# Three PSUM places shared by second stage, exponents and inverse in an S4 layer, and a new order of its rounds

## The chip, the cores and the metric

The kernel runs on one core of a Trainium2 chip. The metric is device time in microseconds (us) of one execution of the program; of several runs the median counts. The engines of the core work side by side, each through its own queue in order: PE (TensorE, matmuls), DVE (VectorE), ACT (ScalarE), POOL (GpSimd) and SP (SyncE, which here only starts DMAs). They wait for one another by semaphores.

## The reference

One layer: an adaptive layer norm, a state space convolution (S4), a second adaptive layer norm, a gated feed-forward. L = 2048 positions, D = 640 channels, N = 128 states, F = 1728.

```
mod = (silu(c) @ w_mod) split into sa, ca, ga, sb, cb, gb
h = layernorm(x) * (1 + ca) + sa
K[d, l] = Re sum_n C[d,n] * exp(dt[d] * A[d,n] * l) * dt[d] * B[d,n]       # l = 0..2047
y = irfft(rfft(h, 4096) * rfft(K, 4096))[:2048] + h * Dskip                # per channel
x = x + ga * y
h = layernorm(x) * (1 + cb) + sb
x = x + gb * ((silu(h @ w1) * (h @ w3)) @ w2)
```

All of it is in float32; the change lies in the part that makes K and convolves.

## The kernel before, in words

The core has 8 PSUM banks of 128 partitions x 512 floats. In the part at issue they are six places: A, B and Z of two banks each, and two single ones, `pk` and `pb`.

The program has three parts. First come the modulation, the first norm and the first DFT stage of h, which goes to DRAM (`us`); its order is a written list of words, FRONT. Then come the rounds, where K is made and the convolution runs. Then come the second norm and the feed-forward, where PE multiplies nearly without a pause.

The rounds work on 40 steps of 16 channels. What they issue is set by a list of words, ROUND, which is run once for each of 10 rounds; the word `E1+2` in round r issues the piece E1 of step 4r + 2, unless it was issued before. On PE, DVE, ACT and POOL pieces stay in the order of the words. The pieces of a step:

- `PH` (POOL, for two steps): phases, three integer operations on the tile `ph`. `AB`, `CO`, `SI` (ACT, for two steps): absolute value, cosine and sine of them, 128x2048.
- `PA`, `PQ` (PE): exponents of the fast and the slow half, two banks each, tile `pa`; `XA`, `XQ` (ACT): their exponentials, into the table `A`.
- `E1`, `E2`, `A1`, `A2` (DVE): tables times cosine (tile `E`) and times sine (tile `A`), 128x1024 and 128x512.
- `kg` (PE): the 64 small matmuls that give 16 channels of K, in `pk`; `K` (DVE): two operations, the skip term added to a column of `pk` and a product into SBUF; `pt` (PE) and `uk` (ACT): the first DFT stage of K, through `pb`.

A channel chunk of 128 has 8 steps. The convolution runs on 40 groups (5 chunks x 8 groups of frequencies), ten steps behind; group words carry the number of the step beside which they run, so `st10` is the first group and `st49` the last:

- `st` (PE): the second DFT stage of h and K, 16 matmuls into two banks, tile `p2`; `kc` (ACT): copies K's half out of it.
- `T` (two operations on DVE): the products, the second of them written back into `p2`; `Y` (DVE): their sums.
- `iv` (PE): the first inverse stage, 16 matmuls; `zt` (ACT): copies its result out for a store.

Before the change `st` goes to place A (odd groups near the end to B), the exponents of all steps from 12 on go to B, and the inverse of two groups fills Z, from which one `zt` of 128x1024 takes both. The names in the profile are `p` for `p2`, `pz`, `pa`, `pk`, `pt`, `kc`, `zt`. Line 115 is a helper that records nearly every operation, so the rows are told apart by tiles.

Beside the words the round loop loads and sums the last columns of the modulation (`LS`, `LP`, `LC`, `LO`, once in each of rounds 2 to 6), loads four tiles of x (`x_load`), and loads what is stored of the first inverse stage (tiles `A<-zs`, `z_load`, on POOL's queue). After the rounds a loop over `tk` runs the groups 42 to 49. At the end of it the first four tiles of x are finished; in the feed-forward they are stored to DRAM on POOL's queue (`xs<-xm`), while four further tiles are loaded (`x_get`) and finished (`x_mid`) beside the first matmuls.

## Time and profile before

| what | value |
|---|---|
| median of three runs | 930.04 us (928.35 to 930.1) |
| profiled execution | 928.49 us |
| its span | 926.6 us |
| PE busy in the span | 865.7 us, 93% |
| DVE, ACT, POOL busy | 696.6, 541.4, 290.7 us |
| mean granted TensorE clock | 0.97 |

The profiled execution lies 1.89 us above its span: that is what lies around the profiled instructions. In a timeline a row has the start, the duration in us, the engine, and in square brackets the idle time ahead of it and whose signal ended it. In windows each engine has its busy time and its number of instructions in a stretch. A duration runs from start to end of one instruction; where the next one is ready, it starts some 0.1 us before that end.

### The profile page before, as it was taken

The page shows a single profiled execution, that of the slowest core. Times are in us where ns is not written, and L with a number is a line of the kernel's source. Part 1 is how long each engine was busy: PE and PEld are TensorE (multiplying, and loading weights), DVE is VectorE, ACT ScalarE, POOL GpSimd, SP SyncE. Part 2 cuts the span into 40 slices and gives each one's busy share as a digit, 9 for nine tenths or more (in the row PEclk, how much of TensorE's full clock was granted, in tenths as well). Part 3 has the DMA queues.
Part 4 walks back from the last instruction along what each step waited for, and adds up shares of the span by engine and source line. Part 5 has one row for each costly group of instructions (what it writes and reads, how often), then busy time and mean ns, then how long its engine had stood idle before and what let it go on. Part 6 is the DMA issues. An engine that isn't in the chain of part 4 may idle for free.

```text
span 926.6 us, 20179 instructions
## 1 busy us (share of the span) xinstructions
PE 865.7 (93%) x8082; PEld 664.7 (72%) x8082; DVE 696.6 (75%) x1210; ACT 541.4 (58%) x746; POOL 290.7 (31%) x327
## 2 busy tenths in 40 slices
PE   3788979999998899899999999999999999999997
PEld 2545556666666677678888887778888888888886
DVE  5899899999999968667666656777976666664664
ACT  5989889999999643474433333574633333333432
POOL 3333535543545212213222202310422222100563
PEclk9777699999999999999999999999999999999999
DMA  8664475766675977953221129946321322123352
GB/s 264 214 221 174 155 214 170 224 176 190 177 222 172 290 225 222 263 189 100 57 58 57 47 82 244 267 128 202 111 58 45 112 57 58 57 86 99 100 188 97
DMA packets 103329, 140.69 MB, mean 152 GB/s; under 512 B 19940, under 2 KB 62436, under 8 KB 103236
## 3 DMA queue, kind: packets, MB, share of 16 engines
q1 hardware_dynamic: 92532, 113.71, 40.8%
q10 hardware_dynamic: 8272, 18.16, 6.7%
q0 software_dynamic: 2432, 7.54, 2.6%
q8 instruction: 63, 1.03, 0.5%
q14 instruction: 30, 0.25, 0.1%
HBM read 107.92 MB, written 31.46 MB: 150 GB/s over the span
## 4 chain that ended last, share of the span: by engine, by line
PE 77%; DVE 10%; ACT 7%; DMA 3%; issue 3%; SPq 0%; POOL 0%; DVEq 0%; ACTq 0%
PE ps L115 56%; PE p L115 7%; PE pz L115 4%; PE pt L115 3%; PE pk L115 2%; PE pa L115 2%; DVE u L115 2%; DVE A L115 2%; DVE uk L115 1%; ACT A L115 1%; ACT cs L115 1%; ACT uk L115 1%; DVE E L115 1%; DMA s<-in_s_dram 1%; DVE st L115 1%
## 5 line engine op out<-in xcount | busy, mean ns | idle before, releaser
L115 DVE TENSOR_TENSOR s<-ps,s 128x512 f32<-128x512 f32 x138 | 94.8, 687 | 82.4 <-PE ps L115 82.0
L115 ACT CAST gh<-rw 128x640 fp32r<-128x640 f32 x87 | 63.3, 727 | 110.2 <-PE ps L115 90.6
L115 DVE TENSOR_TENSOR gl<-rw,gh 128x640 fp32r<-128x640 f32 x87 | 77.3, 888 | 64.1 <-ACT gh L115 64.1
L115 POOL TENSOR_TENSOR S<-rw 128x256 f32<-128x256 f32 x46 | 35.6, 776 | 233.9 <-DVE S0l L115 156.6
L115 POOL TENSOR_TENSOR ph<-thi,iota 128x1376 int32<-128x1376 int32 x20 | 51.3, 2563 | 117.3 <-DVE A L115 96.0
L115 PE MATMUL ps<-xA,gh 128*128 128x512 f32 x280 | 87.5, 391 | 0.4 <-ACT xA L115 0.4
L115 PE MATMUL ps<-gh,uh 128*128 128x512 f32 x224 | 87.4, 390 | 0.0
L115 PE MATMUL ps<-gl,uh 128*128 128x512 f32 x224 | 87.2, 389 | 0.0
L115 PE MATMUL p<-uk,s 128*64 128x256 f32 x576 | 71.1, 389 | 15.1 <-issue 4.2
L115 DVE TENSOR_TENSOR E<-A,cs 128x1024 f32<-128x1024 f32 (+1 forms) x80 | 81.7, 1033 | 3.1 <-PE pk L115 1.8
L115 PE MATMUL ps<-gh,ul 128*128 128x512 f32 x208 | 81.0, 390 | 0.0
L115 ACT ACTIVATE A<-pa 128x1024 f32<-128x1024 f32 (+1 forms) x80 | 64.2, 815 | 10.1 <-PE pa L115 9.5
L115 PEld LDWEIGHTS p<-uk,s 128*64 128x64 f32 x576 | 41.0, 137 | 36.4 <-DVE Y L115 5.6
L115 PEld LDWEIGHTS ps<-xA,gh 128*128 128x128 f32 x280 | 52.3, 188 | 12.6 <-ACT s L115 1.2
L115 POOL TENSOR_TENSOR rw<-rw,gbr 128x128 f32<-128x128 f32 x56 | 36.8, 691 | 72.5 <-DMA rw<-in_w_dram 71.0
L115 DVE TENSOR_TENSOR A<-A,ph 128x1024 f32<-128x1024 f32 x40 | 54.1, 1356 | 0.8
L115 PE MATMUL ps<-xA,gl 128*128 128x512 f32 x140 | 54.5, 389 | 0.0
L115 PE MATMUL pt<-s,K 128*64 128x128 f32 x640 | 46.5, 290 | 5.5 <-ACT uk L115 5.5
L115 PEld LDWEIGHTS ps<-gh,uh 128*128 128x128 f32 x224 | 42.0, 188 | 9.0 <-DVE h L115 0.2
L115 PEld LDWEIGHTS ps<-gl,uh 128*128 128x128 f32 x224 | 42.1, 188 | 8.8
L115 ACT ACTIVATE s<-ps 128x512 f32<-128x512 f32 (+1 forms) x33 | 19.7, 597 | 47.2 <-PE ps L115 47.2
L115 PEld LDWEIGHTS pt<-s,K 128*64 128x64 f32 x640 | 36.8, 144 | 14.0 <-ACT uk L115 8.8
(224 smaller groups left out, 2210.8 us busy)
## 6 DMA issues: line engine op xcount, KB each, us to landing
rw<-in_w_dram ACTq DMA_DIRECT2D x44, 320.0 KB, 3.1
us<-u SPq DMA_DIRECT2D x16, 640.0 KB, 3.4
rw<-in_wg_dram SPq DMA_DIRECT2D x31, 320.0 KB, 2.9
s<-in_s_dram SPq DMA_DIRECT2D x36, 256.0 KB, 4.6
i<-in_i_dram SPq DMA_DIRECT2D x36, 256.0 KB, 4.3
rw<-in_wu_dram SPq DMA_DIRECT2D x28, 320.0 KB, 3.1
uk<-us SPq DMA_DIRECT2D x16, 512.0 KB, 4.9
zs<-zt SPq DMA_DIRECT2D x16, 512.0 KB, 4.5
```

Of the source, the lines that this page charges most:

```text
L115: ins = fn(*args, **kw)
```

## The change

1. `two_banks` hands out the places A, Z and B. A tile of `st`, `PA`, `PQ` (and three tiles of the end) takes the place whose holder was released first; the holder of an exponent is released by its exponential, that of a second stage by its `zt`.
2. The inverse of a group goes into the first half of its own `p2`, and each group has a `zt` of its own, 128x512 instead of 128x1024 for two; the store still takes two.
3. `T` is split into `T` and `P`, and `K` into `D` and `K`, so that they can be put apart.
4. ROUND is rewritten, and the last rounds have a list of their own, LAST.
5. `x_load` moves from the `E1` words of rounds 7 and 8 to `uk` words of rounds 6 and 7; the first twelve `z_load` move behind the rounds; the four stores `xs<-xm` move behind the last `x_mid`; the scale of the modulation is added when a column is copied.

```diff
-            ps = to[s] = psS.tile([P, 2, 512], F32, name="pa", tag="AB"[s % 2] if s < 12 else "B", bufs=1)
+            if s < 12:
+                ps = psS.tile([P, 2, 512], F32, name="pa", tag="AB"[s % 2], bufs=1)
+            else:
+                ps = two_banks([P, 2, 512], "pa", ("XA" if n == NB else "XQ", s))
+            to[s] = ps
+    banks = {"A": ("zt", LAG), "Z": None, "B": None}
+    used = {}
+    def two_banks(shape, name, release):
+        free = [t for t, r in banks.items() if r is None or r in used]
+        tag = min(free, key=lambda t: used.get(banks[t], -1))
+        banks[tag] = release
+        return psS.tile(shape, F32, name=name, tag=tag, bufs=1)
...
-        p2 = psS.tile([P, 2, 2, 2 * DC], F32, name="p2", tag="B" if n > NS - 12 and n % 2 else "A", bufs=1)
+        if n:
+            p2 = two_banks(shape, "p2", ("zt", n + LAG))
+        Zq[ch, g] = p2[:, :, 0].rearrange("p r (i d) -> p r i d", i=2)
...
-        if g % 2 == 0:
-            Zq[ch] = psS.tile([P, 2, 4, DC], F32, name="pz", tag="Z", bufs=1)
-        pz = Zq[ch]
+        pz = Zq[ch, g]
...
+    def k_direct(s):
+        pk = PK[s]
+        keep(V.tensor_tensor(pk[:, :, 0], pk[:, :, 0], dz[:, s * 4:s * 4 + 4], op=OP.add))
+    def products2(ch, g):
+        p2, kc, T = Pq[ch, g]
+        T2 = p2[:, :, :, DC:]
+        keep(V.tensor_tensor(T2, bc(p2[:, :, 1, :DC], 2, 2), kc[:, :, ::-1, :], op=OP.mult))
...
-            return
-        zt = fp.tile([P, 8, DC], F32, name="zt", bufs=2)
-        acopy(zt.rearrange("p (i r) d -> p r i d", r=2), Zq.pop(ch))
+            ztp[0] = fp.tile([P, 8, DC], F32, name="zt", bufs=2)
+        zt = ztp[0]
+        z_out(zt[:, g % 2 * 4:g % 2 * 4 + 4], ch, g)
...
     ROUND = (
-        "E1+2 pt+0 CO+4 kg+1 A1+2 kc+2 SI+4 T+2 PA+4 uk+0 XA+4 Y+2 E2+2 st+3 K+1 zt+1 kc+3 A2+2 kg+2 "
...
+        "PQ+7 LS+4 LP+4 st+5 A1+4 E2+5 XQ+7 PH+8 LC+4 LO+4 CO+6 A1+5 A2+5 kg+4 pt+3 D+4 kc+5 iv+4 SI+6 uk+3 "
...
+    LAST = (
+        "st+37 XQ+38 D+35 E2+37 kc+37 A1+36 D+33 T+37 E1+36 A1+37 pt+34 PQ+39 pt+35 PQ+36 iv+36 kg+36 A1+34 "
...
-            if name == "E1" and 30 <= k < 38 and k % 2 == 0:
-                x_load((k - 30) // 2)
+            if name == "uk" and 28 <= k < 32:
+                x_load(k - 28)
             if name == "kg" and 36 <= k < 40:
                 early.append((None, z_tile()))
-                z_load(early[-1][1], k - 36, range(3), q=nc.gpsimd)
...
+        if tk <= NS + 4:
+            z_load(early[tk - NS - 1][1], tk - NS - 1, range(3), q=nc.gpsimd)
...
-            if pair == 0 and n == 1:
-                with tc.issue_after(power.ins):
+            if pair == 0 and n == 3:
+                with tc.issue_after(kept_out[0].ins):
                     for j, (x, z, st) in enumerate(early):
                         G.dma_start(xs[j], x)
```

What it moves, at three places. First DVE, in a middle round, behind the `A2` that closes step 15. Before:

```order
L115 SCALAR_TENSOR_TENSOR A<-ph,A 128x16x32
L115 TENSOR_TENSOR T<-p_1823,kc 128x512
L115 TENSOR_TENSOR p_1823<-p_1823,kc 128x4x128
L115 TENSOR_TENSOR Y<-T,p_1823 128x2x128 x2
L115 TENSOR_TENSOR A<-A,ph 128x16x64
L115 TENSOR_TENSOR pk<-pk,dz 128x4
L115 TENSOR_TENSOR K_1998<-pk,gaT 128x256
L115 TENSOR_TENSOR E<-A,cs 128x16x64
L115 TENSOR_TENSOR T<-p_1986,kc 128x512
```

And now:

```order
L115 SCALAR_TENSOR_TENSOR A<-ph,A 128x16x32
L115 TENSOR_TENSOR E<-A,cs 128x16x64
L115 TENSOR_TENSOR T<-p_1822,kc 128x512
L115 TENSOR_TENSOR p_1822<-p_1822,kc 128x4x128
L115 TENSOR_TENSOR pk<-pk,dz 128x4
L115 TENSOR_TENSOR Y<-T,p_1822 128x2x128 x2
L115 TENSOR_TENSOR K_1984<-pk,gaT 128x256
L115 TENSOR_TENSOR E<-A,cs 128x16x64
L115 TENSOR_TENSOR T<-p_1972,kc 128x512
```

The operations are the same; a table product `E` now stands directly behind `A2`, the next `A` behind the products has left this place, and the skip term stands between product and sum.

Then ACT, where a round's sines and cosines are. Before:

```order
L115 ACTIVATE ph<-ph 128x32x64
L115 COPY kc<-p_2440 128x512
L115 ACTIVATE cs<-cs 128x2048
L115 COPY uk<-pt 128x32x16
L115 ACTIVATE cs<-ph 128x2048
L115 ACTIVATE cs<-cs 128x2048
L115 COPY kc<-p_2530 128x512
L115 ACTIVATE ph<-ph 128x32x64
L115 COPY uk<-pt 128x32x16
L115 ACT_TABLE_LOAD
L115 ACTIVATE A<-pa 128x16x2x32
L115 COPY zt<-pz 128x2x4x128
```

And now:

```order
L115 ACTIVATE cs<-cs 128x2048
L115 COPY kc<-p_2040 128x512
L115 ACTIVATE ph<-ph 128x32x64
L115 COPY uk<-pt 128x32x16
L115 ACTIVATE cs<-ph 128x2048
L115 COPY zt<-p_1972 128x2x2x128
L115 COPY kc<-p_2128 128x512
L115 ACTIVATE ph<-ph 128x32x64
L115 COPY zt<-p_2040 128x2x2x128
L115 ACTIVATE cs<-cs 128x2048
L115 ACT_TABLE_LOAD
L115 ACTIVATE A<-pa 128x16x2x32
```

Each long one now has one or two copies behind it, and the copies out of the inverse are single groups out of `p`.

Last PE, around the late columns `pm` of a round. Before:

```order
L115 MATMUL p_2781<-uk,s_2779 64x256 x8
L115 MATMUL pa<-r_98,lx 128x512 x2
L115 MATMUL pz<-Y,i_2796 128x128 x8
L115 MATMUL pa<-r_99,lx 128x256 x2
L115 MATMUL pm<-xw,sc 32x384 x4
L115 MATMUL pm<-xw,sc 32x192 x2
L115 MATMUL p_2838<-uk,s_2836 64x256 x8
```

And now:

```order
L115 MATMUL p_2768<-uk,s_2766 64x256 x8
L115 MATMUL pa<-r_98,lx 128x512 x2
L115 MATMUL pt<-s_74,K_2697 64x128 x8
L115 MATMUL p_2617<-Y,i_2804 128x128 x8
L115 MATMUL pa<-r_99,lx 128x256 x2
L115 MATMUL pm<-xw,sc 32x384 x4
L115 MATMUL pm<-xw,sc 32x192 x2
L115 MATMUL p_2836<-uk,s_2834 64x256 x8
```

The inverse now writes into the tile of its own second stage (`p_2617`), and a `pt` stands ahead of it.

More of the change, by code (lines that the diff above doesn't have):

```diff
@@ L470, in late_out @@
         lo, hi = late_blocks[i]
-        keep(V.tensor_copy(modTf[:, 3 * i + lo:3 * i + hi], pm[:, 384 + lo:384 + hi]))
+        for one in (0, 1):
+            c = [b for b in range(lo, hi) if (KD <= 3 * i + b < 2 * KD) == bool(one)]
+            if c:
+                to, src = modTf[:, 3 * i + c[0]:3 * i + c[-1] + 1], pm[:, 384 + c[0]:384 + c[-1] + 1]
+                keep(V.tensor_scalar(to, src, 1.0, None, op0=OP.add) if one else V.tensor_copy(to, src))
         if i >= 3:
             keep(V.tensor_copy(gbr[:, (i - 3) * 256:(i - 3) * 256 + 256], pm[:, :256]))
-        if i == 4:
-            keep(V.tensor_scalar(modT[:, 1, :], modT[:, 1, :], 1.0, None, op0=OP.add))
     hpz = pre.enter_context(tc.tile_pool(name="hpz", bufs=2, side="right"))
@@ L639, in imag2 @@
         A = AA[s]
-        keep(V.scalar_tensor_tensor(A[:, :, 0, :], ph.pop(s)[:, :, 2 * NA - 1:NA - 1:-1], -1.0, A[:, :, 0, :],
+        keep(V.scalar_tensor_tensor(A[:, :, 0, :], ph[s][:, :, 2 * NA - 1:NA - 1:-1], -1.0, A[:, :, 0, :],
                                     op0=OP.mult, op1=OP.mult))
@@ L722, in stage2 @@
         n = ch * 8 + g
-        p2 = psS.tile([P, 2, 2, 2 * DC], F32, name="p2", tag="B" if n > NS - 12 and n % 2 else "A", bufs=1)
+        shape = [P, 2, 2, 2 * DC]
+        if n:
+            p2 = two_banks(shape, "p2", ("zt", n + LAG))
+        else:
+            p2 = psS.tile(shape, F32, name="p2", tag="A", bufs=1)
+        Zq[ch, g] = p2[:, :, 0].rearrange("p r (i d) -> p r i d", i=2)
         for pi in range(2):
@@ L890, in x_products @@
             if j == 2:
-                pys.append(psS.tile([P, 2, 512], F32, name="py", tag="B", bufs=1))
+                pys.append(two_banks([P, 2, 512], "py", ("py", 0)))
             py = [pys[0][:, hh, (j - 2) * 256:] for hh in range(2)]
@@ L933, in do @@
             assert (name, k) not in done and lo <= k < hi, (name, k)
-        if (name, k) in done or not lo <= k < hi or (name == "zt" and k % 2 == 0 and k < LAG + 8 * NDC - 8):
+        if (name, k) in done or not lo <= k < hi:
             return None
         done.add((name, k))
+        used[name, k] = len(used)
         return (conv if name in conv else parts)[name](k)
@@ L1028, in tile_kernel @@
     ROUND = (
[5 rows of a table removed]
[5 rows of a table added]
+    ).split()
+    LAST = (
[8 rows of a table added]
     ).split()
@@ L1036, in tile_kernel @@
     pieces = {"LS": late_sums, "LP": late_part, "LC": late_cols, "LO": late_out}
-    for rnd in range(NS // EB):
+    for rnd in range(8 + 1):
         if 2 <= rnd < 7:
             late_load(rnd - 2)
-        for word in ROUND:
-            name, k = word[:2].rstrip("+-"), EB * rnd + int(word[len(word[:2].rstrip("+-")):])
+        for word in ROUND if rnd < 8 else LAST:
+            name, k = word.split("+")
+            k = int(k) + (EB * rnd if rnd < 8 else 0)
             if name in pieces:
@@ L1070, in tile_kernel @@
         do("zt", tk - 1)
-        do("T", tk)
-        do("Y", tk)
+        for name in "TPY":
+            do(name, tk)
         if tk == NS + 1:
@@ L1096, in tile_kernel @@
             if i == 6:
-                pl = psS.tile([P, 2, 512], F32, name="pl", tag="A", bufs=1)
+                pl = two_banks([P, 2, 512], "pl", ("pl", 0))
                 pls += [pl[:, 0], pl[:, 1]] + [psS.tile([P, 512], F32, name="pl", tag=t, bufs=1) for t in ("pk", "pb")]
@@ L1103, in tile_kernel @@
                 late_products(7)
-    ps = psS.tile([P, 2, 512], F32, name="ps", tag="Z", bufs=1)[:, 0]
+    ps = two_banks([P, 2, 512], "ps", ("ps", 0))[:, 0]
     for _ in range(IDLE):
@@ L1187, in behind @@
         return tc.issue_after(last.ins) if last else ExitStack()
+    kept_out = [None]
     def x_mid(j, got, g):
```

25 lines of the change are left out of this document (15 added, 10 removed), and 15 rows, old and new, of tables (LAST, ROUND).

## The prediction

> **What bounds the kernel now.** I read the windows first, cut at the same `st` of each round (length, then busy time and instructions of PE, weight loads, DVE, ACT and POOL, then clock, DMA share and GB/s), then the groups by form, then one round in order of time, on DVE beside POOL.
>
> ```profile
> 179.80:206.90 27.10, 25.41 (x484) 18.35 (x486) 25.52 (x43) 25.64 (x27) 13.03 (x7) 1.00 0.67 194
> 234.30:261.40 27.10, 25.50 (x480) 18.09 (x480) 25.87 (x45) 25.65 (x27) 12.98 (x7) 1.00 0.63 182
> 261.40:288.10 26.70, 23.56 (x465) 17.21 (x465) 25.20 (x41) 25.25 (x27) 13.35 (x8) 1.00 0.64 204
> 335.50:366.70 31.20, 31.20 (x465) 21.78 (x466) 23.71 (x60) 11.41 (x20) 8.40 (x16) 1.00 0.70 215
> ```
>
> A round with late columns takes 27.1 us, one without 26.7, and in both three engines are within 1.2 to 3.1 us of full. No order makes a round shorter than its fullest engine: DVE 25.5 to 25.9, ACT 25.6. So a reordering can win about 1.5 us in a round, not more. From 335 us on PE has no gap; what is won before that moves the rest up, and nothing there gives it back.
>
> ```profile
> L115 DVE TENSOR_TENSOR T<-p,kc 128x512 f32<-128x512 f32 x24 | 16.4, 685 | 4.9 <-ACT kc L115 4.9
> L115 ACT ACTIVATE A<-pa 128x1024 f32<-128x1024 f32 x22 | 22.6, 1028 | 4.5 <-PE pa L115 4.5
> L115 ACT COPY kc<-p 128x512 f32<-128x512 f32 x23 | 13.4, 582 | 3.2 <-issue 2.5
> L115 ACT COPY zt<-pz 128x1024 f32<-128x1024 f32 x12 | 12.1, 1011 | 0.3
> L115 ACT ACTIVATE cs<-cs 128x2048 f32<-128x2048 f32 x11 | 21.1, 1915 | 0.2
> L115 PE MATMUL p<-uk,s 128*64 128x256 f32 x368 | 44.8, 385 | 10.6 <-DVE Y L115 3.3 <-ACT uk L115 3.2 <-PE pa L115 1.6
> ```
>
> These groups are from 165 to 320 us. DVE's one large wait is for `kc`, the copy behind a second stage; ACT waits for exponents; PE waits ahead of a second stage, for `Y` in part. All three are waits for a PSUM place or follow from one: `st` may not start before the last `Y` has read A, an exponent not before the last was taken out of B.
>
> **The rounds.** DVE and POOL in one round:
>
> ```profile
> 231.82 2.51 POOL L115 TENSOR_TENSOR ph<-thi,iota 128x1376 int32<-128x1376 int32 x1 [5.21 <-DVE A L115]
> 234.41 1.50 POOL L115 TENSOR_TENSOR ph<-ph,phi 128x256 int32<-128x256 int32 x1
> ...
> 234.12 1.29 DVE L115 TENSOR_TENSOR E<-A,cs 128x1024 f32<-128x1024 f32 x1
> 235.51 1.48 DVE L115 TENSOR_TENSOR A<-A,ph 128x1024 f32<-128x1024 f32 x1
> 237.74 0.69 DVE L115 TENSOR_TENSOR T<-p,kc 128x512 f32<-128x512 f32 x1 [0.74 <-ACT kc L115]
> 243.34 0.16 DVE L115 TENSOR_TENSOR pk<-pk,dz 128x4 f32<-128x4 f32 x1
> 243.54 0.42 DVE L115 TENSOR_TENSOR K<-pk,gaT 128x256 f32<-128x256 f32 x1
> 243.88 1.22 DVE L115 TENSOR_TENSOR A<-A,ph 128x1024 f32<-128x1024 f32 x1
> 245.01 1.22 DVE L115 TENSOR_TENSOR E<-A,cs 128x1024 f32<-128x1024 f32 x1
> 246.75 0.68 DVE L115 TENSOR_TENSOR T<-p,kc 128x512 f32<-128x512 f32 x1
> 247.46 0.70 DVE L115 TENSOR_TENSOR p<-p,kc 128x512 f32<-128x512 f32 x1
> 248.20 0.75 DVE L115 TENSOR_TENSOR Y<-T,p 128x256 f32<-128x256 f32 x2
> 248.87 1.69 DVE L115 TENSOR_TENSOR A<-A,ph 128x1024 f32<-128x1024 f32 x1
> ...
> 246.97 2.50 POOL L115 TENSOR_TENSOR ph<-thi,iota 128x1376 int32<-128x1376 int32 x1 [8.52 <-DVE A L115]
> ```
>
> A table product takes 1.22 us (243.88, 245.01) unless POOL is at a phase: then 1.29, 1.48 and 1.69, in all 0.8 a round, which counts as busy. The 1.69 is exact: POOL's phase ends at 249.47, and DVE's row ends 1.09 behind that. DVE stood until POOL's instruction was over. (The Trainium skill, "SBUF — State Buffer", section "Who interferes with whom", says of a VectorE instruction with two SBUF inputs and a GpSimd one that reads SBUF that whichever starts first holds the port and the other blocks. The trace agrees, by the 1.09 us left.)
>
> For the new order I laid the five queues side by side by hand, each instruction at the later of its engine's turn and its inputs, with the start-to-start times of these rows: a table product 1.13, T 0.71, the second product 0.74, Y 0.67, D 0.20, K 0.34, A2 0.61.
>
> *Collisions.* POOL's first phase waits for the `A2` of every second step. An `E1` now stands right behind that `A2`, begins first, and POOL begins 1.1 later. DVE goes on with T, P, D, Y, K (2.7), POOL with its first phase (2.5), and the next `E1` meets only the short second phase, which in the row at 234.41 ran the last 0.5 of its 1.50, the rest being its own wait for DVE: 0.45. Behind the other such `A2` of a round stand D, T, K, P, Y, again 2.7, and the `E1` after them comes as the first phase ends: 0.1. Together 0.5 for 0.8, so -0.3.
>
> *Idle.* DVE idles 27.10 - 25.87 = 1.2 in the round with late columns shown, 1.6 in the other and 1.5 in the last. In the walk, counted from the end of the `A2` of a round's last step but one, the `T` of the three next groups stand at 5.3, 12.3 and 16.0 us, and their `kc` are done at 4.5, 10.7 and 15.8; the `kg` that a `D` needs is done over 1 us ahead each time. So at most the third waits, 0 to 0.4, and the short gaps between dependent rows stay, some 0.4: I take 0.8. Bounds: 0.3 (gaps alone) and 1.5 (as now). The split of the modulation's copies adds one small row, 0.07.
>
> *Round.* DVE's mean busy 25.7 - 0.3 + 0.07 + 0.8 = 26.3 for 27.1: -0.8 in each of five rounds with late columns. Without: 25.2 - 0.3 + 0.8 = 25.7 for 26.7: -1.0 in one. The six come to **-5.0**. Both other engines must stand it. PE: 25.5 of 26.3. ACT: two `zt` of 1011 ns become four that I cost as a `kc` copy of the same shape (582), +0.3, so 26.0 of 26.3. This copy is hidden only as long as ACT's 1.45 of idle shrink to 0.3; if they stay, the round is 27.4.
>
> **The entry.** The front is unchanged up to `st10`.
>
> ```profile
> 123.24 1.95 PE L115 MATMUL p<-uk,s 128*64 128x256 f32 x16 [0.21 <-ACT uk L115]
> 130.12 2.91 PE L115 MATMUL p<-uk,s 128*64 128x256 f32 x16 [2.60 <-issue]
> ...
> 122.72 2.50 POOL L115 TENSOR_TENSOR ph<-thi,iota 128x1376 int32<-128x1376 int32 x1 [6.43 <-ACT cs L115]
> ...
> 123.64 2.67 DVE L115 TENSOR_TENSOR E<-A,cs 128x1024 f32<-128x1024 f32 x1
> 129.27 0.75 DVE L115 TENSOR_TENSOR Y<-T,p 128x256 f32<-128x256 f32 x2
> 134.78 0.17 DVE L115 TENSOR_TENSOR pk<-pk,dz 128x4 f32<-128x4 f32 x1 [1.29 <-PE pk L115]
> 137.59 0.68 DVE L115 SCALAR_TENSOR_TENSOR A<-ph,A 128x512 f32<-128x512 f32 x1
> ```
>
> Now `st11` waits at 130.12 for the `Y` that ends at 130.02, since both use A; `kg10` is queued behind it on PE, and DVE waits 1.29 for `kg10` at 134.78. With a place of its own `st11` starts right behind `pt8` and its exponents, some 2.6 earlier, `kg10` no longer waits for it, and the 1.29 go. The `A1` behind the first `E1`, now 1.49 beside POOL, comes after T, D, P, K, Y and is free: 0.3. With gaps I take **-1.8** at the `A2` of step 11 (137.59); bounds -1.3 and -2.6.
>
> **The last rounds.**
>
> ```profile
> 300.40 0.69 DVE L115 SCALAR_TENSOR_TENSOR A<-ph,A 128x512 f32<-128x512 f32 x1
> 328.93 0.42 DVE L115 TENSOR_TENSOR K<-pk,gaT 128x256 f32<-128x256 f32 x1
> ...
> 333.33 1.04 PE L115 MATMUL pt<-s,K 128*64 128x128 f32 x16
> 334.30 1.16 PE L115 MATMUL pz<-Y,i 64*128 64x128 f32 x16
> 335.39 1.95 PE L115 MATMUL p<-uk,ph 128*64 128x256 f32 x16
> ```
>
> The row at 300.40 is the `A2` of step 35; from 137.59 to it are six rounds, 162.8 us or 27.1 each. The last `K` ends at 329.3, and `st42`, which needs all of chunk 4, starts at 335.39: behind that `K` stand `st41`, `pt39` and an `iv`, 6.1 us. LAST puts T, P, Y of group 40 and T of 41 (0.71 + 0.73 + 0.67 + 0.71 = 2.8) ahead of the last `K`, and behind it only `pt39` (1.0) and an `iv` (1.1) with a signal: 2.2. That is +2.8 - 3.9 = -1.1, if DVE idles as before. From 301.0 to 329.3 it has seven table products, eight short ones, five groups of T, P and Y and five of D and K (7.9 + 4.9 + 10.6 + 2.7 = 26.1), which leaves 2.2 idle; with the `kc` of groups 38 to 41 ready earlier I take 1.3. **-2.0**; bounds -1.1 and -2.6.
>
> **The tail** from `st42` on stays: PE is full, `st` and `iv` alternate, and three places for groups that each last a turn and a half suffice. The twelve `z_load` now stand behind the rounds in the program, but on POOL nothing is ahead of them. At nothing: the tables of groups 42 to 45 are fetched early and cover them.
>
> **The feed-forward's start.**
>
> ```profile
> 371.23 2.48 POOL L115 DMA_DIRECT2D xs<-xm  x4
> 388.68 0.85 PE L115 MATMUL ps<-A,i 64*32 64x384 f32 x8 [1.18 <-DMA A<-zs]
> 394.65 0.85 PE L115 MATMUL ps<-A,i 64*32 64x384 f32 x8 [0.91 <-DMA A<-zs]
> 366.70:396.00 29.30, 25.13 (x163) 17.64 (x164) 20.64 (x48) 12.55 (x17) 9.89 (x21) 1.00 1.04 276
> ```
>
> PE waits twice for loads, 2.1 us, with the DMA engines full (share 1.04, 276 GB/s). The four stores of 320 KB issued at 371.23 are 4.7 us of that traffic and now come behind the loads. Bounds 0 and -2.1; nearer to the second: **-1.5**. Behind 396 us PE is full for the rest.
>
> **Sum** against the profiled execution: 928.49 - 1.8 - 5.0 - 2.0 - 1.5 = 918.2. It lies 1.55 under the median of the runs; with half of that, 919.0.
>
> **Rivals.** *ACT becomes the bound*: its rounds keep their idle, 27.4 instead of 27.1, +2.0 over six, and only the other terms remain: 928.5 + 2.0 - 5.3 = 925.2, or 926 by the median. For it: 26.0 of 26.3 is very full. Against: its idle is for `pa`, which gets more places.
>
> *Slower: places held too long.* A second stage now keeps its two banks until `zt`, and a round claims three places twelve times. Where a `zt` is queued behind one more cosine (1915 ns), the next claim waits, and PE with all behind it. Two such claims a round cost 3.8; PE has 27.1 - 25.4 = 1.7 to spare, and beyond that it decides: +2.1 a round, +12.6 in six, less 5.3: 937 by the median. For it: PE's queue is in order, and claims are by release order, not by need. Against: in my walk the claims of a round wait under 1 us in all.
>
> *Slower: collisions.* The worst row is 2.67 (123.64, DVE behind a POOL phase that began first). If both phase pairs of a round cost 1.45 each instead of 0.8 together, that is +2.1, or +12.6 in six, less some 0.55 of idle in each and the 5.3: 933. Against: the walk has DVE first, or POOL nearly done, in each meeting. (The rule of the Trainium skill's page "SBUF — State Buffer" above speaks for it: whoever loses the race pays up to the other's whole instruction, and the walk's margins are 0.1 to 0.2 us.)
>
> *Late loads collide with the tail*: the twelve loads run among the tail's `s2` tables. A table's buffer is free when the `st` two groups ahead ends, so it has an `st` (1.95) and two `iv` (1.16 each), 4.2 us. Two tables that need twice that cost 4.2 each: 919 + 8 = 927. Against: the loads can start as soon as POOL is idle, well ahead of the last four groups.
>
> *No effect in sum*: 929.5.
>
> **Chances.** Forecast 0.52; ACT 0.20; late loads 0.08; no effect 0.07; places 0.09; collisions 0.04. A difference under 0.2%, 1.9 us, cannot be told from none. So faster 0.80, same 0.07, slower 0.13. The likeliest case alone runs from 914 (all lower bounds: -2.6, -8.0, -2.6, -2.1) to 926 (all upper: -1.3, -0.8, -1.1, 0). The range for 8 in 10 takes in ACT, late loads and no effect and leaves out most of the slower ones: 913 to 931.
>
> **What would show it.** Right: `T` without waits of 0.7 for `kc`; rounds of 25.7 to 26.4 between every fourth `st`; no table product beside POOL over 1.7; `st11` near 127.5; `st42` near 326.5; PE without DMA waits from 380 to 396. Wrong: waits of PE ahead of `st` or `pa` that name ACT's `zt` (places), ACT busy over 98% of a round of 27 (ACT), `E` or `A` rows over 2 us in each round (collisions), PE waiting for `s` tables behind 330 (late loads).

## The result, and the profile after

The changed kernel takes 919.3 us in the median of 6 runs (917.02 to 920.7), the kernel before 929.19 us (6 runs, 927.44 to 935.19): a ratio of 0.9886, 95% interval 0.9868 to 0.9904. The profiled execution took 918.55 us with a span of 916.6, against 928.49 and 926.6. So 10.0 us went, where 10.3 had been forecast; but they did not all go where the forecast had them.

| stretch of the profiled execution | before | after | change | forecast |
|---|---|---|---|---|
| start to the `A2` of step 11 | 137.59 | 135.35 | -2.24 | -1.8 |
| from there to the start of `st42` | 197.80 | 189.09 | -8.71 | -7.0 |
| from there to the first `ps<-xA` | 39.54 | 39.16 | -0.38 | 0 |
| from there to the end | 551.67 | 553.0 | +1.3 | -1.5 |

**The rounds.** The windows of the changed kernel, cut at every fourth `st` (length, then busy time and instructions of PE, weight loads, DVE, ACT, POOL, then clock, DMA share and GB/s):

```profile
154.62:179.86 25.24, 25.14 (x484) 17.89 (x482) 24.58 (x44) 25.18 (x29) 12.19 (x6) 1.00 0.67 208
179.86:206.10 26.24, 25.31 (x485) 18.03 (x483) 25.10 (x43) 25.57 (x29) 12.19 (x6) 1.00 0.69 198
206.10:231.90 25.80, 25.18 (x482) 17.69 (x480) 24.88 (x44) 25.33 (x29) 12.22 (x6) 1.00 0.72 202
231.90:256.95 25.05, 24.92 (x482) 17.52 (x480) 24.11 (x44) 24.93 (x29) 12.19 (x6) 1.00 0.70 223
256.95:282.10 25.15, 23.48 (x466) 16.81 (x464) 24.36 (x42) 25.09 (x29) 12.99 (x8) 1.00 0.55 172
```

and the first and the last of these rounds in the kernel before:

```profile
158.81:185.89 27.08, 25.34 (x483) 18.31 (x483) 25.50 (x43) 25.63 (x27) 13.01 (x6) 1.00 0.65 194
267.13:294.31 27.18, 23.55 (x465) 17.18 (x465) 26.37 (x41) 25.73 (x27) 12.65 (x7) 1.00 0.53 158
```

The four rounds with late columns take 25.6 us in the mean, where they took 27.1; the one without takes 25.15, where its counterpart at the same `st` took 27.18. DVE's busy time fell from 25.7 in the mean of the four to 24.7, a whole microsecond under what the prediction had taken for a floor, and ACT's fell too, from 25.6 to 25.25, though it has two copies more. In the first and the fourth of these rounds PE is busy to within 0.13 us of the length; in the one without late columns ACT is. In these three hardly any slack is left; the second and the third are 0.7 and 0.5 us longer than their fullest engine is busy, and in each PE has a stall that the last section comes back to.

The groups by form from 165 to 320 us (count, busy time and mean ns of one, idle time ahead and what ended it), of the changed kernel:

```profile
L115 DVE TENSOR_TENSOR A<-A,ph 128x1024 f32<-128x1024 f32 x24 | 29.2, 1217 | 0.1
L115 DVE TENSOR_TENSOR T<-p,kc 128x512 f32<-128x512 f32 x25 | 17.1, 685 | 1.6 <-ACT kc L115 1.4
L115 ACT ACTIVATE A<-pa 128x1024 f32<-128x1024 f32 x21 | 22.5, 1072 | 0.1
L115 ACT COPY zt<-p 128x512 f32<-128x512 f32 x25 | 14.6, 587 | 1.1 <-PE p L115 1.0
L115 POOL TENSOR_TENSOR ph<-thi,iota 128x1376 int32<-128x1376 int32 x9 | 25.9, 2882 | 57.5 <-DVE pk L115 28.8 <-ACT kc L115 21.9 <-DVE A L115 6.8
```

and two rows of the same view of the kernel before:

```profile
L115 DVE TENSOR_TENSOR A<-A,ph 128x1024 f32<-128x1024 f32 x23 | 32.6, 1417 | 0.6
L115 POOL TENSOR_TENSOR ph<-thi,iota 128x1376 int32<-128x1376 int32 x10 | 25.0, 2504 | 68.4 <-DVE A L115 68.4
```

A product `A<-A,ph` takes 1217 ns where it took 1417, and POOL's first phase 2882 where it took 2504: the stalls have changed sides. A stall of POOL should cost nothing here, since POOL is idle half of the round; whether a stall of DVE costs something is tested below. The waits of the prediction's list are nearly gone as well: `T` for `kc` 1.6 us instead of 4.9, ACT for exponents 0.1 instead of 4.5.

How it looks in one round, DVE and POOL in order of time (start, duration; in brackets the idle time ahead and what ended it):

```profile
238.18 1.22 DVE L115 TENSOR_TENSOR E<-A,cs 128x1024 f32<-128x1024 f32 x1
238.41 3.36 POOL L115 TENSOR_TENSOR ph<-thi,iota 128x1376 int32<-128x1376 int32 x1 [7.33 <-ACT kc L115]
241.78 1.22 DVE L115 TENSOR_TENSOR E<-A,cs 128x1024 f32<-128x1024 f32 x1
...
250.28 0.68 DVE L115 SCALAR_TENSOR_TENSOR A<-ph,A 128x512 f32<-128x512 f32 x1
251.11 2.51 POOL L115 TENSOR_TENSOR ph<-thi,iota 128x1376 int32<-128x1376 int32 x1 [5.96 <-DVE pk L115]
253.28 1.42 DVE L115 TENSOR_TENSOR E<-A,cs 128x1024 f32<-128x1024 f32 x1
```

At 238.18 DVE's product begins first and runs its 1.22 us; POOL's phase, asked for 0.2 later, reads 3.36 and ends at 241.77, and the next product begins at 241.78. Between the two lie the short products T, P, D, Y and K. At 253.28 the product still meets the last 0.3 of a phase and reads 1.42. That is all that is left of 0.8 us a round.

**The entry.** PE and DVE, and the clock (0.50) in a window of 2 us:

```profile
122.94 3.68 PE L115 MATMUL p<-uk,s 128*64 128x256 f32 x16
129.25 1.95 PE L115 MATMUL p<-uk,s 128*64 128x256 f32 x16
...
122.00:124.00 2.00, 2.00 (x46) 1.45 (x39) 0.89 (x3) 2.00 (x2) 2.00 (x1) 0.50 1.05 255
...
135.35 0.68 DVE L115 SCALAR_TENSOR_TENSOR A<-ph,A 128x512 f32<-128x512 f32 x1
```

`st10` takes 3.68 us instead of 1.95 because the granted clock is 0.50 then; `st11` comes at 129.25, not at 127.5, and DVE's `T` at 127.28 waits 1.72 for the `kc` behind the slow `st10`. The waits named in the prediction are gone all the same (no wait of 1.29 for `kg10` is left), and the `A2` of step 11 is 2.24 earlier, 0.30 of which was there before `st10`. That gain doesn't hang on what `st10` does: in seven of the kernels of the next section, which have the same order here, `st10` starts between 122.60 and 124.79, in four of them at full clock, and that `A2` between 133.70 and 135.47.

**The last rounds.** PE's `st39`, the last `K` on DVE, and `st42`:

```profile
306.34 1.95 PE L115 MATMUL p<-uk,s 128*64 128x256 f32 x16 [1.94 <-DMA s<-in_s_dram]
...
321.48 0.42 DVE L115 TENSOR_TENSOR K<-pk,gaT 128x256 f32<-128x256 f32 x1
...
324.44 4.96 PE L115 MATMUL p<-uk,ph 128*64 128x256 f32 x42
```

From the last `K` to `st42` are 2.96 us where there were 6.46. `st39` waits for a table, which nobody had forecast.

**The feed-forward's start.** PE, ACT and POOL:

```profile
384.09 0.92 ACT L115 ACTIVATE T<-xm,rs 128x640 f32<-128x640 f32 x1 [6.32 <-POOL rs L115]
...
386.21 0.71 ACT L115 CAST gh<-rw 128x640 fp32r<-128x640 f32 x1
386.97 0.74 PE L115 MATMUL ps<-xA,gh 128*128 128x512 f32 x2 [2.29 <-ACT gh L115]
...
388.57 0.56 POOL L115 DMA_DIRECT2D xs<-xm  x1
391.21 0.20 POOL L115 TENSOR_TENSOR rs<-rs,epst 128x1 f32<-128x1 f32 x1
391.45 0.92 ACT L115 ACTIVATE T<-T,rs 128x640 f32<-128x640 f32 x1 [2.65 <-POOL rs L115]
392.43 1.20 PE L115 MATMUL ps<-ident,T 128*128 128x128 f32 x9 [1.02 <-ACT T L115]
```

and ACT in the kernel before:

```profile
395.40 0.93 ACT L115 ACTIVATE T<-xm,rs 128x640 f32<-128x640 f32 x1 [6.31 <-POOL rs L115]
...
401.63 0.92 ACT L115 ACTIVATE T<-T,rs 128x640 f32<-128x640 f32 x1 [2.14 <-POOL rs L115]
```

PE waits for no load any more, as forecast. It waits 2.29 us for a cast of weights instead, which stands on ACT behind two `T` that wait for POOL, and 1.02 for the last `T`, since the moved stores are now issued between the four small operations of the last tile's statistics. Counted from the first `ps<-xA`, the first of these `T` comes at +20.49 here and at +20.47 in the kernel before (395.40, behind the first `ps<-xA` at 374.93), and the last one at +27.85 where it came at +26.70 (401.63): the loads had been waited for beside a chain that ended as late anyway, and the moved stores made that chain 1.15 us longer.

### The profile page after: what moved, and what is told of

Same layout as the page of the kernel before. It is cut to its first block, busy times and chain, and to the rows that moved or that the text cites. A ratio compares the mean times of both kernels' runs of the same rounds, so it can differ in the third digit from the quotient of the medians.

```text
span 916.6 us, 20217 instructions
## 1 busy us (share of the span) xinstructions
PE 865.5 (94%) x8082; PEld 662.8 (72%) x8082; DVE 685.2 (75%) x1210; ACT 537.6 (59%) x762; POOL 283.8 (31%) x327
## 3 DMA queue, kind: packets, MB, share of 16 engines
q8 instruction: 63, 1.03, 0.5%
## 4 chain that ended last, share of the span: by engine, by line
PE 56%; ACT 1%; DVE 0%; DVEq 0%; issue 0%; ACTq 0%
PE ps L115 56%; DVE xm L115 0%; ACT T L115 0%; ACT xm L115 0%; ACT gh L115 0%; ACT idle L115 0%; ACT s L115 0%; DVEq L1760 0%; ACT uh L115 0%; DVE ul L115 0%; ACT xA L115 0%; ACTq L115 0%; DVEq L115 0%
## 5 line engine op out<-in xcount | busy, mean ns | idle before, releaser
L115 POOL TENSOR_TENSOR ph<-thi,iota 128x1376 int32<-128x1376 int32 x20 | 56.3, 2816 | 112.4 <-DVE pk L115 34.4
L115 DVE TENSOR_TENSOR A<-A,ph 128x1024 f32<-128x1024 f32 x40 | 48.5, 1217 | 0.1
L115 PE MATMUL pk<-A 128*32 128x64 f32 x1280 | 43.7, 233 | 4.1 <-DVE A L115 2.0
```

The source lines that it names most:

```text
L115: ins = fn(*args, **kw)
```

## The experiments

The theory after the result: in the rounds, the stalls of DVE behind POOL's phases were the larger half of the gain, and the order took them away; the three places only make that order possible. In the feed-forward's start, a chain over DVE, POOL and ACT sets the end, not the loads. The rivals: the places won the rounds and the order only follows; ACT is now the bound; the loads do matter there.

**One product begun beside a phase.** The cheapest test of the first: no work added, one word moved.

```diff
-        "AB+8 T+5 st+6 zt+4 K+4 P+5 Y+5 E1+6 kc+6 ...
+        "AB+8 T+5 E1+6 st+6 zt+4 K+4 P+5 Y+5 kc+6 ...
```

> The changed kernel with one word of the round moved: the E1 behind the T, K, P and Y that follow the first A2 of a pair now stands right behind that T, so that it begins while POOL is at its first phase; no work is added. Theory DVE (a table product that begins beside a phase stands until the phase ends, and DVE sets the round): this E1 reads 2.5 to 3.2 us instead of 1.42 once a round, DVE's busy time grows by 1.2 to 1.8 a round, and since DVE has 0.9 us to spare in a round, the round grows by 0.5 to 1.5, the whole by 4 to 11 us (923 to 930). Theory ACT and PE (they are 99% full and set the round, DVE's stalls are free): the row shows the stall, but the round grows by under 0.3, the whole by under 2.

Measured: 930.04 us, 1.0006 of the kernel before (0.9984 to 1.0028). One word takes back the whole gain. POOL and DVE in one round, and the window of that round:

```profile
202.54 2.50 POOL L115 TENSOR_TENSOR ph<-thi,iota 128x1376 int32<-128x1376 int32 x1 [5.62 <-DVE pk L115]
202.98 3.14 DVE L115 TENSOR_TENSOR E<-A,cs 128x1024 f32<-128x1024 f32 x1
...
183.66:210.45 26.79, 24.96 (x484) 17.76 (x482) 26.26 (x43) 25.34 (x29) 12.19 (x6) 1.00 0.67 196
```

The product ends at 206.12, 1.08 us behind the end of POOL's phase at 205.04: it stood for 1.92 us in all. DVE is busy 26.26 of 26.79. The round takes 26.8 to 28.7 with late columns (the longest has a granted clock of 0.94), 26.3 without, 1.7 more than in the changed kernel in the mean of five. So DVE's stalls are not free, and a single one a round is worth what the change won. One thing is mixed in: `K` now stands behind the whole 3.14 us of that product, and PE waits 1.50 for it in this round. What the later place of `K` would cost without the stall, no run separates. (The Trainium skill's page "SBUF — State Buffer", section "Who interferes with whom", says that whichever of the two instructions starts first keeps the shared port to its end and the other blocks; the 1.08 us left of a product of 1.22 agree.)

**The places with the old order.** The changed kernel's code, places and copies, with the words of the kernel before in every round; `zt` of a group right behind its `iv`, but for one that keeps its old place.

```diff
-    ROUND = ("PQ+7 LS+4 LP+4 st+5 ...
-    LAST = ("st+37 XQ+38 ...
+    ROUND = ("E1+2 pt+0 CO+4 kg+1 ... T+2 P+2 ... iv+2 zt+2 ... iv+3 kc+4 XA+7 E1+5 PQ+7 zt+3 ...
+             "... iv+4 zt+4 K+4 Y+5 st+6 iv+5 zt+5 AB+8 "        # all ten rounds
```

> The three shared places, the inverse in its second stage's place, the copies zt by group, the split copies of the modulation and the late loads as in the changed kernel, but all rounds in the order of the kernel before (zt of a group right behind its iv). Theory order (the rounds were won by DVE's products standing so that POOL's phases run beside the short ones): the collisions stay, A<-A,ph of 128x1024 near 1.45 us as before, only the waits for kc shrink; rounds 26.3 to 26.7 us between every fourth st, against 25.0 to 26.2 of the changed kernel, and the whole 924 to 927. Theory places (PE and ACT no longer wait for PSUM, the order only follows): rounds within 0.3 us of the changed kernel's mean of 25.6, the whole 919 to 921.5. If the old order meets too few places, PE waits for ACT's zt and rounds are over 27.

Measured: 961.35 us, 1.0347 of the kernel before (1.0324 to 1.037); from `st` to fourth `st` 31.4 to 33.9 us. Both theories were far off. The last `zt` of a round stood ahead of an Abs and a cosine on ACT and waited there for its `iv`, and `kc` came late behind them all, so that DVE waited 4.2 to 4.6 us for it. That could have been my placing of `zt`, so the next run puts each `zt` behind the work that stood ahead of such a copy in the kernel before (the edit is against the run above).

```diff
-  "... A1+2 kc+2 SI+4 ...  K+1 kc+3 ...  iv+2 zt+2 PA+6 ... AB+6 PQ+6 ...  iv+4 zt+4 ... iv+5 zt+5 AB+8 "
+  "... A1+2 kc+2 zt+0 SI+4 ...  K+1 zt+1 kc+3 ...  iv+2 PA+6 ... AB+6 zt+2 PQ+6 ...  iv+4 ... iv+5 AB+8 "
```

> As e3_old_order, but each zt behind the work that the kernel before had there (the one of the last group of a round not ahead of the Abs, but behind K; that of the group ahead of it behind kc; the first behind the next Abs), so that ACT no longer waits for an iv ahead of a long row. Theory order: the collisions stay (A<-A,ph near 1.45), the T of a round's first group still waits for its kc, which stands behind an Abs and a cosine on ACT; rounds 26.3 to 27.2, the whole 925 to 930, so the places alone win under half of the change's 10 us. Theory places: rounds 25.6 to 26, the whole 919 to 922. Over 930: more places without the order are a loss.

Measured: 974.93 us, 1.0468 (1.0443 to 1.0492), worse still. PE's waits from 165 to 300 us, four rounds (sum, times, longest), then one `st` and the window behind it:

```profile
PE p L115 <- ACT A L115: 14.6, 4, 3.7
PE p L115 <- ACT zt L115: 7.6, 4, 1.9
...
195.10 3.68 PE L115 MATMUL p<-uk,s 128*64 128x256 f32 x16 [3.73 <-ACT A L115]
...
196.00:198.00 2.00, 2.00 (x12) 1.18 (x10) 0.00 (x0) 0.00 (x0) 0.00 (x0) 0.50 0.64 262
```

This is the prediction's rival of places held too long, in full: a second stage claims the place that an exponent holds, the exponent stands on ACT behind 2 us rows, and PE waits 3.73 and once more 1.90 in each round. Behind the first wait the clock is 0.50 and the `st` itself takes 3.68. So the three places are no gain by themselves; with the old order, in the two placings of `zt` that were tried, they are a loss of 32 and 44 us. The order without the places was not tried, and it could not be taken over as it stands: in its list the `st` of one group stands ahead of the `P` and `Y` of the group before, which still read the place that this `st` had in the kernel before. So what the order alone would bring stays open.

**One step of the order in the kernel before.** What can be tried there is a single collision.

```diff
-  "... E2+3 K+2 pt+2 A1+3 E1+4 A2+3 T+3 PQ+5 uk+2 Y+3 XQ+5 "
+  "... E2+3 A1+3 E1+4 A2+3 T+3 PQ+5 Y+3 K+2 pt+2 uk+2 XQ+5 "
```

> The kernel BEFORE with one step of its round moved and nothing else (its own three fixed places, its own order): K of the third step, with its pt and uk, stands behind the Y that follows the second A2 of a pair, so that T, P, Y and K (2.7 us) lie beside POOL's first phase and the A1 behind them meets it no more. Theory order by itself (one collision of 0.47 a round goes, and DVE sets the round): that A1 reads 1.22 us instead of 1.69, the rounds 26.5 to 26.7 us instead of 27.08, the whole 3 us below the kernel before (926). Theory chain (the round of the kernel before is set by st waiting for Y and T for kc, through places, and DVE's saved time turns into a longer wait for kc): the row falls to 1.22, DVE's waits grow by as much, rounds within 0.15 us of 27.08, the whole within 1 us of the kernel before.

Measured: 978.27 us, 1.0525 of the kernel before (1.05 to 1.0551). DVE and PE:

```profile
204.36 1.22 DVE L115 TENSOR_TENSOR A<-A,ph 128x1024 f32<-128x1024 f32 x1
...
204.49 1.92 PE L115 MATMUL pt<-s,K 128*64 128x128 f32 x16 [2.65 <-DVE K L115]
...
209.81 0.17 DVE L115 TENSOR_TENSOR pk<-pk,dz 128x4 f32<-128x4 f32 x1 [4.24 <-PE pk L115]
```

The collision is gone, 1.22 for 1.69, as meant. But `pt` waits 2.65 us for the `K` that now comes later, and the inverse, the next exponents and the next `kg` stand behind it on PE; DVE's next D then waits 4.24 for that `kg`. To save 0.47 a round on DVE, 5 to 7 us were lost through PE's queue: from `st` to fourth `st` the rounds take 32.3 to 34.4 us for 27.1. Neither theory had this. Taken out in this way, a collision costs far more than it saves, so the gain from removing stalls alone was not measured by any run; the new order moved the queues together.

**Is ACT the bound now?** The cosine on half of its columns takes 1.9 us of a round from ACT; what this kernel leaves out is the cosine of the other half, which goes on as bare angles.

```diff
-        act(c, c, AF.Sin, scale=-2 * math.pi / TURN, bias=math.pi / 2)
+        h = c[:, :SD] if s >= 12 else c
+        act(h, h, AF.Sin, scale=-2 * math.pi / TURN, bias=math.pi / 2)
```

> The changed kernel with the cosine taken on only half the columns from step 12 on (the other half goes on as bare angles, so this part of the result is left out): ACT has 1.9 us less in each round, all else is the same. In the changed kernel's rounds ACT is busy 24.9 to 25.6 us of 25.05 to 26.24, PE 24.9 to 25.3 where there are late columns and 23.5 where there are none, DVE 24.1 to 25.1. Theory ACT (ACT is now the bound): the round without late columns falls from 25.15 to 24.2 to 24.5, those with them to PE's 25.1, the whole by 2.5 to 5 us to 914.5 to 917. Theory DVE and PE (the chain of products and of matmuls sets the round, ACT only keeps pace): every round within 0.3 us of the changed kernel's, the whole within 1.5 us of 919.

Measured: 916.42 us, 0.9848 (0.9816 to 0.9879), some 3 us below the changed kernel, but the two intervals overlap. A round with late columns and the one without:

```profile
230.93:255.98 25.05, 24.92 (x482) 17.52 (x480) 23.58 (x43) 23.58 (x29) 12.21 (x6) 1.00 0.68 223
255.98:280.40 24.42, 23.25 (x466) 16.68 (x465) 24.14 (x42) 23.73 (x29) 12.44 (x7) 1.00 0.54 174
```

With late columns the fourth round stays at 25.05 although ACT and DVE are both 1.5 us short of it: PE is the bound there, 24.92 of 25.05. Without them the round falls from 25.15 to 24.42, so ACT had been the bound in it, and DVE is next. Of 1.9 us less on ACT the rounds with late columns give back 0.1 us in the mean (25.46 for 25.58), no more than kernels with the very same rounds differ by (25.4 to 25.6). The theory that ACT is the bound holds for the rounds without late columns alone.

**The late loads at their old places.**

```diff
-            if name == "uk" and 28 <= k < 32:
-                x_load(k - 28)
+            if name == "E1" and 30 <= k < 38 and k % 2 == 0:
+                x_load((k - 30) // 2)
             if name == "kg" and 36 <= k < 40:
                 early.append((None, z_tile()))
+                z_load(early[-1][1], k - 36, range(3), q=nc.gpsimd)
```

> The changed kernel with the four x loads and the twelve loads A<-zs on POOL issued at the places of the kernel before (the x loads beside E1 of steps 30 to 36, the A<-zs loads beside kg of steps 36 to 39 within the rounds). The prediction costed their move at nothing. Theory nothing: POOL's loads start between 281 and 303 us in both kernels whatever their place in the program, st42 stays within 0.5 us of 324.4, the whole within 1 us of the changed kernel (918.5 to 920.5). Theory queue (where they stand decides which load comes late): PE's wait of 1.94 us for the table s ahead of the st at 306.34 goes or doubles, the whole moves by 2.

Measured: 920.58 us, 0.9907 (0.9882 to 0.9932). PE:

```profile
306.98 3.68 PE L115 MATMUL p<-uk,s 128*64 128x256 f32 x16 [3.34 <-DMA s<-in_s_dram]
```

The wait for the table is 3.34 instead of 1.94, the `st` behind it runs at half clock, and from `st35` (281.59 here, 282.10 in the changed kernel) to `st42` (326.08 here) are 44.5 us instead of 42.3; four more kernels of this section with these loads at the new places take 41.5 to 42.7. By the whole times the two kernels can't be told apart; by the stretch, one trace for each, the move of these loads is worth about 2 us, not nothing.

**The feed-forward's start: three kernels against one chain.** First the four stores back where they were.

```diff
-            if pair == 0 and n == 3:
-                with tc.issue_after(kept_out[0].ins):
+            if pair == 0 and n == 1:
+                with tc.issue_after(power.ins):
```

> The changed kernel with one part undone: the four stores xs<-xm of the first tiles go out again behind the statistics' power (beside the second plain block), not behind the last x_mid. Theory A (the wait for loads in the kernel before hid a chain on DVE, POOL and ACT that ends at the same time in both; what the moved stores did is to stand on POOL's queue between the small operations of the last tile's statistics, 1.15 us): PE waits for A<-zs about 2.1 us in the feed-forward's start again, but its transposes behind the third plain block start 1.1 us earlier than in the changed kernel; from the first ps<-xA to the end 551.7 to 552.0 us instead of 553.0, the whole 917.3 to 918.5. Theory B (the prediction: the stores' traffic delays the loads, and the loads hold PE): the stretch grows by 1.5 to 554.5, the whole to 921.

Then the stores as late as the changed kernel has them, but behind the last of the small operations.

```diff
-        G.tensor_tensor(rs[:, 3:4], rs[:, 2:3], epst[:, 2:3], op=OP.mult)
+        last_rs[0] = G.tensor_tensor(rs[:, 3:4], rs[:, 2:3], epst[:, 2:3], op=OP.mult)
...
-                with tc.issue_after(kept_out[0].ins):
+                with tc.issue_after(last_rs[0].ins):
```

> The changed kernel with the four stores xs<-xm issued behind the last small operation of the last tile's statistics on POOL, instead of between them. Theory A: T of the last tile is ready 1.1 us earlier, PE's wait of 1.02 for it goes, the wait of 2.29 for the cast gh stays; the stretch from the first ps<-xA to the end is 551.9, the whole 1.1 us shorter than the changed kernel (918.2). Theory B (these waits are noise beside the loads): no change, within 0.3 us.

Then, with that, the casts of the fourth plain block ahead of the two `T` on ACT.

```diff
-            ws = ws or plain_weights(f, ends if pair == 0 and n == 1 else None)
+            ws = ws or (early_w.pop(0) if early_w else plain_weights(f, ends if pair == 0 and n == 1 else None))
...
+            if pair == 0 and n == 1:
+                early_w += [plain_weights(f) for f in simple[2:]]
+                norm_behind[0] = last_cast[0]
             beside(end)
+            norm_behind[0] = None
...
-        S.activation(xn, x, AF.Identity, scale=rstd, bias=bias)
+        with tc.issue_after(norm_behind[0].ins) if norm_behind[0] else ExitStack():
+            S.activation(xn, x, AF.Identity, scale=rstd, bias=bias)
```

> As e2_stores_later, and the casts gh and uh for the fourth plain block stand ahead of the two x_norm operations T on ACT, not behind them. Theory A (what PE waits for in the changed kernel at 386.97 is ACT's queue: the casts behind two T that wait for POOL's small operations): the wait of 2.29 us goes, the low clock behind it in e2_stores_later (0.79 and 0.50 in the two windows of 2 us) too; from the first ps<-xA to the first matmul behind the next transposes 26.0 to 27.0 us, against 29.8 in the changed kernel and 28.7 in the one before; the whole 915 to 917. Theory B (another wait takes its place, since DVE's sums and POOL's operations stay as long): the stretch stays over 28.5.

And both the first and the third of these edits: the casts ahead, with the stores back.

> As e1_stores_back, with the casts ahead of the two T on ACT as in e9. Theory A: PE's wait for A<-zs of about 1.8 stays (the stores' traffic is ahead of the loads), and what follows is no longer hidden by it: the stretch from the first ps<-xA to the first matmul behind the transposes 28.0 to 28.6, the whole 916 to 917, no better than e9. Prediction's step (the loads hold PE by 1.5 us more with the stores in front): e10 is 1.5 us above e9.

Measured, with the stretch from the first `ps<-xA` to the first matmul behind the next transposes (each ratio is to runs of the kernel before that were made beside those of the kernel in its row: 929.52 in the median for the two middle rows, 930.88 for the last two):

| kernel | stretch | PE's waits in it | whole | ratio to before (interval) |
|---|---|---|---|---|
| before | 374.93 to 403.59, 28.66 | loads 1.18, 0.91 | 929.19 | |
| changed | 363.60 to 393.38, 29.78 | cast 2.29, `T` 1.02 | 919.3 | 0.9886 (0.9868 to 0.9904) |
| stores back | 362.71 to 391.35, 28.64 | load 1.82 | 916.87 | 0.9876 (0.9847 to 0.9904) |
| stores later | 362.48 to 392.33, 29.85 | cast 2.28 | 918.78 | 0.9887 (0.9866 to 0.9907) |
| stores later, casts first | 362.10 to 387.63, 25.53 | none | 913.25 | 0.9808 (0.9779 to 0.9838) |
| stores back, casts first | 361.98 to 392.01, 30.03 | loads 0.79, 1.05 | 918.71 | 0.9863 (0.984 to 0.9887) |

With the stores back, PE waits for the load and the transposes go at 390.01, 27.30 behind the start (27.44 in the kernel before):

```profile
377.26 0.85 PE L115 MATMUL ps<-A,i 64*32 64x384 f32 x8 [1.82 <-DMA A<-zs]
...
390.01 1.58 PE L115 MATMUL ps<-ident,T 128*128 128x128 f32 x12
```

So the changed kernel's move of the stores was worth +1.1 us in this stretch, as theory A had it, through POOL's queue. By the whole times the two kernels can't be told apart. With the stores later, `T` is in time (no wait of PE for it is left), but the gain doesn't show: behind the wait for the cast the clock fell, and the block that took 3.95 us in the changed kernel (386.97 to 390.92) took 5.29:

```profile
385.82 0.96 PE L115 MATMUL ps<-xA,gh 128*128 128x512 f32 x2 [2.28 <-ACT gh L115]
...
387.00:389.00 2.00, 2.00 (x6) 1.52 (x6) 1.77 (x3) 0.02 (x1) 1.76 (x4) 0.50 0.64 186
```

With the casts first, ACT uses a part of the 6.3 us in which it had waited, and PE doesn't stand at all:

```profile
379.25 0.72 ACT L115 CAST gh<-rw 128x640 fp32r<-128x640 f32 x1
383.12 0.93 ACT L115 ACTIVATE T<-xm,rs 128x640 f32<-128x640 f32 x1 [2.53 <-POOL rs L115]
...
386.41 1.47 PE L115 MATMUL ps<-ident,T 128*128 128x128 f32 x12
```

The stretch is 4.25 us shorter than in the changed kernel, more than theory A had expected, and the whole 913.25 us; its interval and the changed kernel's don't meet. This version beats both kernels. And with the stores back under the same casts, the loads are late again and now it counts:

```profile
381.45 0.85 PE L115 MATMUL ps<-A,i 64*32 64x384 f32 x8 [1.05 <-DMA A<-zs]
...
384.00:386.00 2.00, 2.00 (x6) 1.61 (x5) 1.42 (x4) 1.75 (x3) 0.35 (x2) 0.50 1.01 353
```

30.03 against 25.53: 4.5 us for stores that go ahead of loads, 1.84 of them waits of PE and 1.6 the low clock behind them (the block from 382.23 takes 5.14 us for 3.55). Theory A's expectation for this kernel (28.0 to 28.6) left the clock out. So the prediction's mechanism was true, and the waits that it takes away are near the 2.1 us that it named; it could only not be collected while another chain ended as late.

**The last tables.** A try to collect the wait of `st39` in the same way.

```diff
-            if name == "iv" and 36 <= k < 40:
-                    last_pair(k - 36)
+            if name == "st" and 39 <= k < 43:
+                    last_pair(k - 39)
```

> As e9_casts_first_stores_later, and the loads of the last groups' tables into the phases' places (ph<-in_s_dram, ph<-in_i_dram, two a group) are asked for behind the s load of the second stage three groups later, not beside an iv. In the changed kernel two of them stand on SP's queue ahead of the s load that is issued at 298.79 and lands 7.5 us later, and PE waits 1.94 for it at 306.34. Theory A (a queue's order, as with the casts): that wait goes, st42 about 1.5 to 2 us earlier than in e9 (322.95), the whole 911 to 912. Theory B (the DMA engines are full there, share 0.99, and some table is late in any order): the wait moves to another st, the whole within 0.7 us of e9's 913.25.

Measured: 913.81 us, 0.9854 (0.9816 to 0.9893). PE:

```profile
303.53 1.95 PE L115 MATMUL p<-uk,s 128*64 128x256 f32 x16
312.13 0.25 PE L115 MATMUL pk<-A 128*32 128x64 f32 x2 [2.18 <-issue]
```

`st39` waits no more, 1.4 us earlier than in the kernel with the casts first; but `kg` further on stands 2.18 us for nothing that the profile names (1.37 there) and goes on at 312.13 against 312.16, and `st42` starts at 322.92 against 322.95. Theory A was wrong: the wait was hidden by what comes behind it, and by the whole times the two kernels are the same. What `kg` stands for there is the last point of the last section.

## Why the prediction was right, and where it was not

The time, the sign and the likeliest case were right: 919.3 for 919.0. That the sum of -10.3 met -10.0 so closely is in part luck: two of its terms were off by about as much in opposite ways, the rounds with their end by -1.7 and the feed-forward's start by +2.8; the rest came from the entry and the tail (-0.4 each). Within the first of these lies another such pair: from the `A2` of step 11 to `st35` the kernel won 10.0 us, where six rounds had been put at -5.0, and from `st35` to `st42` it lost 1.3, where -2.0 stood.

*The entry* (-1.8, bounds -1.3 and -2.6): -2.24. The mechanism was right (`st11` right behind `pt8` and its exponents, the 1.29 for `kg10` gone, the first `E1` 1.94 instead of 2.67), though `st11` came at 129.25 and not near 127.5. A clock of 0.50 at `st10` was in no step; a share of 0.30 came from ahead of `st10`, which I had called unchanged.

*The rounds* (-0.8 with late columns, -1.0 without): -1.5 and -2.0, counted at the `st`. The step that failed is "No order makes a round shorter than its fullest engine: DVE 25.5 to 25.9". DVE's busy time is no floor, for two reasons. It held 0.8 us of stalls a round (rows of 1.29, 1.48 and 1.69 for 1.22), of which the prediction took 0.3 off, since the walk left 0.5 of collisions; 0.2 are left (1.42 at 253.28). And rows that follow closely overlap by some 0.1 in these traces, and busy time counts an overlap once: summed row by row, DVE's four rounds with late columns hold 28.1 us each before and 27.5 after, of which 2.4 and 2.8 overlap. So the 1.5 us of such a round are 0.6 of shorter rows, 0.4 of closer rows and 0.5 of idle time (1.4 before, 0.9 now; the 0.8 that I took for it was right). The stalls are the largest of the three and not the larger half, as my theory after the result had it. ACT did not become 26.0 for the same reason: its `zt` cost 587 ns as I had it (582) and its rows add up to 28.4 us for 27.3, but 3.2 of that overlap where 1.7 did. A collision was dearer than I priced it: 1.45 for the worst, and the product begun beside a phase stood 1.92.

*The last rounds* (-2.0): from `st35` to `st42` the changed kernel is no faster (42.3 for 41.1). The step "behind it only `pt39` (1.0) and an `iv` (1.1) with a signal: 2.2" came near: `st42` starts 2.96 behind the start of the last `K`, of which the `K` is 0.42. In the same stretch stand 1.94 us of `st39`'s wait for its table and a stall of `kg` of 1.43, and the step had neither; how much of the lost gain they make up stays open. "At nothing" for the late loads was wrong: back at their old places they cost about 2 us in this stretch.

*The feed-forward's start* (-1.5, bounds 0 and -2.1): +1.3, outside its bounds. The step that failed is "Bounds 0 and -2.1": I looked at PE's waits for loads and not at what else ends at the time when they end. In the kernel before, ACT's `T` at 395.40, the cast at 397.52 and the last `T` at 401.63 stood there to be read, behind POOL's `rs`; PE was held until 394.65 by the load and so never met them. And I moved four issues on POOL without asking what stands behind them on POOL's queue. A loss was possible, and the bound at 0 excluded it without a reason.

*The rivals.* ACT as the bound holds only in rounds without late columns, by 0.7 us. Places held too long: in the changed kernel the waits of PE that name `zt` come to 0.4 us in all, but with the old order they and those for exponents cost 5.6 us a round, where I had priced two claims at 3.8, and the low clock comes on top. Collisions: 933 was the price with both phase pairs of a round, and one product begun beside one phase a round made 930. Late loads against the tail's tables: they met `st39`'s table instead, 1.94 us.

## What to carry to other kernels

Busy time is not work: where two engines stand in each other's way, look for rows of one shape with two durations before calling the fullest engine's busy time a floor. Before costing the removal of a wait, list everything else that must be ready at the moment when it ends, each engine's queue included; whatever is ready at that moment too is the new bound, and removing both may be worth more than either. More buffers pay only together with an order that frees them in time: here the same three places came to -10 us with one order, and to +32 and +44 with the other.
